# Attention plus gated MLP on one core: query blocks outermost, P V as column-tiled matmuls, and a static task-graph schedule

## The chip, the cores and the metric

One core of one Trainium2 chip. The metric is device time in microseconds (us) of the whole program, the median of several runs. The kernel before was run again beside every experiment. Its medians in those calls were 999 to 1001 us, so medians of different calls can be put side by side to about 0.2%; its single runs lie between 994.6 and 1008.4 us. The *clock* of a run is the share of the full TensorE clock that the profile records as granted.

## The reference, cut to what matters

```python
xn = layernorm(x)                                   # x: 1 x 2048 x 512
q, k, v = split(xn @ wqkv)                          # 32 heads of 16
p = softmax(q @ k.T / 4)                            # 32 heads x 2048 x 2048
attn = (p @ v) @ wo
h = relu(xn @ W_gate) * (xn @ W_up)                 # 1792 wide
out = x + attn + h @ W_down
```

The softmax takes 32 x 2048 x 2048 exponentials. Both kernels compute them on ScalarE as 683 activations of 128x1536 straight from PSUM (three PSUM banks, which I call a *unit*), and skip the maximum. A 17th column of ones in v gives the row sums. Everything that is not scores, exp or P V is *background*: projections of q, k, v, the gated MLP and the output projection. It has one PSUM bank in both kernels.

## The kernel before

Heads are taken in groups of four; for one group and one tile of 128 keys, all 2048 queries. P V has exp as the stationary operand (128x128) and v as the moving one (17 columns), and VectorE adds the result into SBUF once per head and key tile:

```python
def issue_partial(p):                  # one head, one key tile, 16 query tiles
    ...
    for m in range(NT):
        ev = PE.op(lambda e, ...: e.matmul(
            ps_pv[:, m, 0:VN], pool[:, sl, off:off + 128], v_aug[:, kt, h, 0:VN], start=True, stop=True), ...)
    ...
        eva = DV.op(lambda e, a=a: e.tensor_tensor(acc[:, a, :, 0:VN], ps_pv[:, :, 0:VN], acc[:, a, :, 0:VN], ALU.add), C_DVE)
```

Each unit issues three row-tiled score matmuls, the exp, at most one P V partial, and then about two background matmuls (a budget of 350 ns at 250 ns each):

```python
for u in range(NU):
    if u >= NS:
        PE.wait(ev_exp[u - NS])
    ...                                                       # three score matmuls, one exp
    if state["next_p"] < len(pending) and p_ulast[pending[state["next_p"]]] <= u - NS:
        issue_partial(pending[state["next_p"]])
        state["next_p"] += 1
    bg_step(u, BG_BUDGET_NS * (n / 3.0))                      # BG_BUDGET_NS = 350
```

The prologue normalises all 2048 rows and transposes them before the first exp.

The softmax here doesn't subtract the row's maximum and nothing guards it: scores larger than these inputs give would overflow.

## Time and profile before

| | us |
|---|---|
| median of the runs | 998.8 |
| profiled run | 1002.1 |
| start of the first exp | 35.6 |
| 683 exps at 1.345 each | 919 |
| time lost between exps | 28 |
| after the last exp | 20 |

The exps (one activation of a unit each) set the pace: in undisturbed stretches one starts every 1.345 us. So I read the kernel as a prologue, 683 exps at that pace, what is lost between them, and a tail.

First the page of the kernel before: span, busy time, two rows of the slices (tenths busy; the tenths of full TensorE clock that were granted), the chain that ended last, and the costliest groups (busy us, mean ns of one | idle time before them, and what ended it).

```profile
span 1002.1 us, 25305 instructions
PE 868.8 (87%) x11424; PEld 372.3 (37%) x11424; DVE 457.2 (46%) x968; ACT 944.0 (94%) x703; POOL 6.4 (1%) x8
...
ACT  5799998999999999999999999999999999999992
...
PEclk9999986899955799699995899899977575555556
...
ACT 70%; PE 21%; DVE 6%; DMA 2%; issue 1%; SPq 0%; DVEq 0%; ACTq 0%
...
L976 ACT ACTIVATE pool<-ps_sc 128x1536 bf16<-128x1536 f32 (+1 forms) x683 | 925.9, 1754 | 21.2 <-PE ps_sc L953 19.1
L917 DVE TENSOR_TENSOR acc<-ps_pv,acc 128x272 f32<-128x272 f32 x480 | 212.6, 443 | 416.0 <-PE ps_pv L904 413.6
L953 PE MATMUL ps_sc<-qTb,kTb 32*128 32x512 bf16 x2048 | 322.4, 465 | 72.4 <-ACT pool L976 68.6
L904 PE MATMUL ps_pv<-v_aug,pool 128*128 128x17 bf16 x8192 | 292.9, 173 | 2.4 <-DVE acc L917 1.7
```

ScalarE is busy 94% of the span and the chain lies on its exps. VectorE is far from full (46%). The clock row falls to half near the end and dips before.

Next, TensorE's part of the timeline: a unit with background work at full clock, then two units without at half clock (start us, duration us).

```profile
601.74 0.39 PE L953 MATMUL ps_sc<-qTb,kTb 32*128 32x512 bf16 x3 [0.41 <-ACT pool L976]
...
602.07 0.56 PE L904 MATMUL ps_pv<-v_aug,pool 128*128 128x17 bf16 x16
...
602.48 0.59 PE L511 MATMUL ps_bg<-xnT,wus 128*128 128x512 bf16 x2
...
603.09 0.39 PE L953 MATMUL ps_sc<-qTb,kTb 32*128 32x512 bf16 x3
```

```profile
860.33 0.61 PE L953 MATMUL ps_sc<-qTb,kTb 32*128 32x512 bf16 x3 [0.21 <-ACT pool L976]
...
860.87 0.59 PE L904 MATMUL ps_pv<-v_aug,pool 128*128 128x17 bf16 x16
...
861.67 0.61 PE L953 MATMUL ps_sc<-qTb,kTb 32*128 32x512 bf16 x3 [0.21 <-ACT pool L976]
```

From the start of a score group to the next matmul it is 0.32 us at full clock and 0.54 at half. In both cases the next score group comes about 1.345 us later.

### The profile page before, as it was taken

The page shows a single profiled execution, that of the slowest core. Times are in us where ns is not written, and L with a number is a line of the kernel's source. Part 1 is how long each engine was busy: PE and PEld are TensorE (multiplying, and loading weights), DVE is VectorE, ACT ScalarE, POOL GpSimd, SP SyncE. Part 2 cuts the span into 40 slices and gives each one's busy share as a digit, 9 for nine tenths or more (in the row PEclk, how much of TensorE's full clock was granted, in tenths as well). Part 3 has the DMA queues.
Part 4 walks back from the last instruction along what each step waited for, and adds up shares of the span by engine and source line. Part 5 has one row for each costly group of instructions (what it writes and reads, how often), then busy time and mean ns, then how long its engine had stood idle before and what let it go on. Part 6 is the DMA issues. An engine that isn't in the chain of part 4 may idle for free.

```text
span 1002.1 us, 25305 instructions
## 1 busy us (share of the span) xinstructions
PE 868.8 (87%) x11424; PEld 372.3 (37%) x11424; DVE 457.2 (46%) x968; ACT 944.0 (94%) x703; POOL 6.4 (1%) x8
## 2 busy tenths in 40 slices
PE   2899988999999999998989998999989987787774
PEld 1333433333343333333343333433334333343332
DVE  7455444455555335443355543445535522332226
ACT  5799998999999999999999999999999999999992
POOL 2000000000000000000000000000000000000000
PEclk9999986899955799699995899899977575555556
DMA  7000211121220002021030110212100000000002
GB/s 262 22 2 3 74 43 48 43 71 45 55 62 1 12 12 65 22 54 23 1 86 1 33 43 2 54 25 52 33 22 2 2 1 1 2 1 1 1 2 85
DMA packets 73532, 34.40 MB, mean 34 GB/s; under 512 B 60240, under 2 KB 71760, under 8 KB 73424
## 3 DMA queue, kind: packets, MB, share of 16 engines
q1 hardware_dynamic: 72272, 31.73, 11.6%
q8 instruction: 90, 1.47, 0.6%
q10 hardware_dynamic: 1152, 1.05, 0.3%
q14 instruction: 18, 0.15, 0.0%
HBM read 25.95 MB, written 6.82 MB: 33 GB/s over the span
## 4 chain that ended last, share of the span: by engine, by line
ACT 70%; PE 21%; DVE 6%; DMA 2%; issue 1%; SPq 0%; DVEq 0%; ACTq 0%
ACT pool L976 70%; PE ps_sc L953 7%; PE ps_pv L904 6%; PE ps_bg L663 2%; PE ps_bg L542 2%; PE ps_bg L524 1%; DVE acc L917 1%; DVE stats L250 1%; PE ps_bg L573 1%; DVE resb L676 1%; PE ps_bg L511 1%; PE ps_bg L639 1%; DVE stg L674 1%; DMA wus<-in_B_W_up_dram 1%; PE psT L286 1%
## 5 line engine op out<-in xcount | busy, mean ns | idle before, releaser
L976 ACT ACTIVATE pool<-ps_sc 128x1536 bf16<-128x1536 f32 (+1 forms) x683 | 925.9, 1754 | 21.2 <-PE ps_sc L953 19.1
L917 DVE TENSOR_TENSOR acc<-ps_pv,acc 128x272 f32<-128x272 f32 x480 | 212.6, 443 | 416.0 <-PE ps_pv L904 413.6
L953 PE MATMUL ps_sc<-qTb,kTb 32*128 32x512 bf16 x2048 | 322.4, 465 | 72.4 <-ACT pool L976 68.6
L904 PEld LDWEIGHTS ps_pv<-v_aug,pool 128*128 128x128 bf16 x8192 | 245.3, 99 | 157.8 <-issue 89.5
L904 PE MATMUL ps_pv<-v_aug,pool 128*128 128x17 bf16 x8192 | 292.9, 173 | 2.4 <-DVE acc L917 1.7
L953 PEld LDWEIGHTS ps_sc<-qTb,kTb 32*128 32x128 bf16 x2048 | 68.6, 94 | 357.0 <-ACT pool L976 287.5
L524 PE MATMUL ps_bg<-xnT,wgs 128*128 128x512 bf16 x224 | 70.9, 399 | 6.6 <-DVE up_sb L518 6.4
L511 PE MATMUL ps_bg<-xnT,wus 128*128 128x512 bf16 x224 | 68.8, 389 | 9.0 <-DVE hT L533 6.9
L542 PE MATMUL ps_bg<-Wd_sb,hT 128*128 128x512 bf16 x224 | 75.2, 421 | 1.0 <-DVE resb L550 1.0
L533 DVE SCALAR_TENSOR_TENSOR hT<-ps_bg,up_sb 128x512 bf16<-128x512 f32 x56 | 38.7, 691 | 20.9 <-PE ps_bg L524 20.8
L518 DVE COPY up_sb<-ps_bg 128x512 f32<-128x512 f32 x56 | 38.7, 691 | 20.7 <-PE ps_bg L511 20.6
L676 DVE TENSOR_TENSOR resb<-ps_bg,resb 128x512 f32<-128x512 f32 x48 | 33.2, 691 | 8.4 <-PE ps_bg L663 8.4
L573 PE MATMUL ps_bg<-xnT,Wk_pad 128*128 128x512 bf16 x96 | 31.7, 415 | 4.8 <-DVE stg L582 4.8
L582 DVE CAST stg<-ps_bg 128x512 bf16<-128x512 f32 x36 | 24.9, 691 | 17.9 <-PE ps_bg L573 7.2
L663 PE MATMUL ps_bg<-Wo_sb,oT_sb 128*128 128x512 bf16 x50 | 29.2, 584 | 2.9 <-DVE resb L676 2.4
L914 DVE COPY acc<-ps_pv 128x272 f32<-128x272 f32 x32 | 14.2, 443 | 26.3 <-PE ps_pv L904 26.1
L286 PE MATMUL psT<-ident,xn_buf 128*128 128x128 bf16 x64 | 9.0, 304 | 19.7 <-DVE xn_buf L278 18.3
L639 PE MATMUL ps_bg<-ident,o_sb 128*64 128x128 bf16 x116 | 22.7, 296 | 0.2
L597 PE MATMUL ps_bg<-Wv_sb,xnT 128*128 128x512 bf16 x64 | 19.2, 382 | 1.8 <-DVE v_aug L603 1.4
L511 PEld LDWEIGHTS ps_bg<-xnT,wus 128*128 128x128 bf16 x224 | 13.2, 97 | 17.7 <-DVE hT L533 11.0
L524 PEld LDWEIGHTS ps_bg<-xnT,wgs 128*128 128x128 bf16 x224 | 13.2, 97 | 14.8 <-DVE up_sb L518 10.2
L570 PE MATMUL ps_bg<-xnT,Wq_perm 128*128 128x512 bf16 x48 | 16.0, 418 | 2.5 <-DVE stg L582 2.5
(59 smaller groups left out, 199.4 us busy)
## 6 DMA issues: line engine op xcount, KB each, us to landing
wgs<-in_B_W_gate_dram SPq DMA_DIRECT2D x56, 128.0 KB, 2.3
wus<-in_B_W_up_dram SPq DMA_DIRECT2D x56, 128.0 KB, 2.8
kT_scr<-stg SPq DMA_DIRECT2D x24, 128.0 KB, 1.8
kTb<-kT_scr SPq DMA_DIRECT2D x6, 512.0 KB, 3.5
x_sb<-in_A_x_dram SPq DMA_DIRECT2D x4, 512.0 KB, 5.7
Wd_sb<-in_B_W_down_dram SPq DMA_DIRECT2D x1, 1792.0 KB, 15.1
wqkv_sb<-in_A_wqkv_dram SPq DMA_DIRECT2D x1, 1536.0 KB, 10.6
qT_scr<-stg SPq DMA_DIRECT2D x12, 128.0 KB, 1.8
```

Source lines behind the costliest of these rows:

```text
L511: fns.append(lambda e, pf, ph, dt=dt, slot=slot, sc=sc: e.matmul(pf, wus[:, slot, dt, :], xnT[:, dt, 512 * sc:512 * (sc + 1)], start=(dt = ...
L518: upj.evac = (lambda e, pf, ph, us=us: e.tensor_copy(up_sb[:, us, :], pf))
L524: fns.append(lambda e, pf, ph, dt=dt, slot=slot, sc=sc: e.matmul(pf, wgs[:, slot, dt, :], xnT[:, dt, 512 * sc:512 * (sc + 1)], start=(dt = ...
L533: gj.evac = (lambda e, pf, ph, us=us, ft=ft: e.scalar_tensor_tensor(out=hT[:, ft, :], in0=pf, scalar=0.0, in1=up_sb[:, us, :], op0=ALU.max ...
L542: fns.append(lambda e, pf, ph, ft=ft, st=st: e.matmul(pf, hT[:, ft, 128 * st:128 * (st + 1)], Wd_sb[:, ft, :], start=(ft == 0), stop=(ft = ...
L573: fns.append(lambda e, pf, ph, dt=dt, idx_=idx_, sc=sc: e.matmul(pf, Wk_pad[:, dt, idx_, :], xnT[:, dt, 512 * sc:512 * (sc + 1)], start=(d ...
L663: return [lambda e, pf, ph: e.matmul(pf, oT_sb[:, tb, mq, 128 * t:128 * (t + 1)], Wo_sb[:, gg, :], start=True, stop=True)]
L676: wj.evac = (lambda e, pf, ph, m=m: e.tensor_tensor(resb[:, m, :], pf, resb[:, m, :], ALU.add))
L904: ev = PE.op(lambda e, m=m, sl=sl, off=off, kt=kt, h=h: e.matmul(ps_pv[:, m, 0:VN], pool[:, sl, off:off + 128], v_aug[:, kt, h, 0:VN], sta ...
L917: eva = DV.op(lambda e, a=a: e.tensor_tensor(acc[:, a, :, 0:VN], ps_pv[:, :, 0:VN], acc[:, a, :, 0:VN], ALU.add), C_DVE)
L953: ev = PE.op(lambda e, bank=bank, kb=kb, qb=qb, j=j, kt=kt, c4=c4: e.matmul(ps_sc[:, bank, :], kTb[32 * j:32 * j + 32, kb, 128 * kt:128 * ...
L976: ev_exp[u] = AC.op(lambda e, s0=s0, n=n, fb=fb: e.activation(pool[:, s0:s0 + n, :], ps_sc[:, fb:fb + n, :], ACTF.Exp, scale=0.25), C_ACT)
```

## The change

Its intent: P V with v as the stationary operand (17 columns, one column tile per head) and exp as the moving one (512 queries), so that four heads sum over all key tiles inside one PSUM bank. That needs query blocks outermost, and it frees VectorE from 480 additions. Everything else is written as operations with dependencies, modelled durations and priorities. A list scheduler orders them once, at build time, and that order is each engine's program. The prologue normalises only the first 512 rows before the first exp. The diff, cut to its core:

```diff
+    def run(self):                     # Graph: the list scheduler
+        ...
+        while n < len(ops):
+            best = None
+            for e in self.ENGS:
+                pick = None
+                for o in cand[e]:
+                    at = earliest(o)
+                    ...
+                    late = at > free[e] + 1e-6
+                    key = (late, at if late else 0.0, o.prio, o.idx)   # ready ones first, then by priority
...
-        def issue_partial(p):
...
-                    ps_pv[:, m, 0:VN], pool[:, sl, off:off + 128], v_aug[:, kt, h, 0:VN], start=True, stop=True),
+                        ins = e.matmul(ps_b[32 * j:32 * j + VN, 0, :], v_aug[:, kt, 8 * gg + 2 * j + ee, 0:VN],
+                                       ring[:, UNIT * tr.slot + i, :], start=(kt == 0), stop=(kt == NT - 1), tile_position=(0, 32 * j))
...
-            bg_step(u, BG_BUDGET_NS * (n / 3.0))
+        for c4 in range(NB):
+            a = upos(c4) + (40 if c4 == 0 else 28)
+            z = upos(c4 + 1) - (12 if c4 < NB - 1 else 50)
+            for ft in range(FT):
+                later(a + (z - a) * ft / FT, 8, lambda pr, od, c4=c4, ft=ft: glu(c4, ft, pr, od))
+            for i in range(4):
+                if c4 < NB - 1:
+                    later(upos(c4 + 1) + 8 + 4 * i, 6, lambda pr, od, c4=c4, i=i: out_rows(c4, i, pr, od, range(8), True, True))
+                else:
+                    later(upos(c4, 3, 1, 0) + 8 + 4 * i, 6, lambda pr, od, c4=c4, i=i: out_rows(c4, i, pr, od, range(7), True, False))
...
+            dma(lambda e: e.dma_start(rsum[:, par, :], o_sb[DH:128:32, to.slot, :]), ...)      # row sums out of the four tiles
+            G.op("DVE", 260, lambda e: e.reciprocal(rrec[:, par, :], rsum[:, par, :]), ...)
+            dma(lambda e: e.dma_start(rec_scr[n].rearrange("j (i q) -> (j i) q", q=16), rrec[:, par, :]), ...)
+                ins = e.dma_start(rb[:, trb.slot, :], rec_scr[n].unsqueeze(1).to_broadcast([4, 32, 512]))
+            G.op("POOL", 1200, lambda e: e.tensor_tensor(oT[:, tn.slot, :], o_sb[:, to.slot, :], rb[:, trb.slot, :], ALU.mult), ...)
```

One query block is 171 units, and there are four. `glu` is 8 matmuls of up and gate; `out_rows` is 22 matmuls (14 of down, 8 of the output projection) for 128 rows.

## The prediction

> **What bounds the kernel now.** ScalarE. In the page's costliest groups the exp (683 activations of 128x1536 from PSUM) is busy 926 of 1002 us; in undisturbed stretches of the chain of waits one starts every 1.345 us (66 in 88.8 us), so the exps alone need 919 us. By the timeline the first exp starts at 35.6 us, the last ends at about 982. The span is 36 (prologue) + 919 + 28 (stalls between exps) + 20 (tail). The waits of ScalarE name score matmuls for 19 of the 28.

> **What the change does.** The exps keep count, shape and pace. Only the other 83 us can move.

> 1. P V. Before: 8192 matmuls, 128x128 weights, 17 columns moving; 16 take 0.56 us, 12 belong to a unit, so about 0.40 us of PE a unit, and 480 additions on VectorE (213 us). After: 2048 matmuls of 512 columns, three in different column tiles. Row-tiled scores show three at once: 0.32 us a group at full clock, 0.54 at half. If column tiles overlap as well [...], P V costs 0.3 us a unit. VectorE loses 200 us of work, but it isn't the bound, so that gives almost nothing directly. PE load at full clock: 0.32 + 0.32 + 0.28 (216 background matmuls of 0.22 us per 171 units) = 0.92 of 1.345 us.
> 2. Background work is spread over the whole run. The granted clock, 0.85 mid-run and 0.5 after 800 us by the windows, should stay at 0.85 or more. At half clock the load would be 1.6 us a unit, over the exp's pace, so cold stretches cost. I expect stalls of 12 us in steady state, down from 28.
> 3. Prologue. LayerNorm in blocks of 512 rows, no late table loads, no permuted weight copies. From measured pieces: x lands at 4.9, four bn_stats 2.4, power on GpSimd 1.2, normalise and transpose 2.5, copy-out 1, q 2, k mask 1.5, score 0.5: first exp at 16.5 instead of 35.6 us, 19 saved.
> 4. But the first 21 units run through all 16 key tiles in 29 us, and VectorE must normalise three more blocks (7.3 us each) and evacuate v (16 x 0.69): about 37 us of VectorE from 4.9 us on, needed by 38. I expect 7 us of stall: part of the prologue comes back.
> 5. Tail: the division now goes through three small DMAs of about 2 us each and a GpSimd multiply, but only four output tiles remain instead of 16: 16 instead of 20 us.

> **Sum.** 16.5 + 919 + 7 + 12 + 16 = 970 as profiled; the median before is 3 us below its profile, so 967 us, 80% range 952 to 985. Faster by over 2%: 0.78; within 2%: 0.17; slower by over 2%: 0.05.

> **What would show the steps.** First exp near 16.5 us; exp waits before 45 us naming k masks or scores; VectorE busy near 250 us; P V groups of three near 0.32 us; clock 0.85 or more to the end; exp pace unchanged; 16 us after the last exp.

> **What would make it wrong.** Column tiles that run one after another (0.65 us a unit: PE bound, over 1000 us). [...] The clock falling to half. A fixed PE order waiting for a late VectorE evacuation of the one P V bank or the one background bank.

Before the run nothing showed that column tiles overlap; the 0.3 us of step 1 was an estimate from the 0.32 us of the score groups. The 1.2 us of step 3 for the power on GpSimd is in no trace of the kernel before; the changed kernel took 1.02 us for it (L448).

## The result, and the profile after

The changed kernel takes 1047.5 us (median of 4) against 1000.9: **4.8% slower** (ratio 1.048, 95% interval 1.044 to 1.052). The prediction was 967 us.

The page of the changed kernel, with the lines that answer to those above:

```profile
span 1044.5 us, 11864 instructions
PE 863.8 (83%) x5152; PEld 205.5 (20%) x5152; DVE 191.1 (18%) x323; ACT 932.4 (89%) x687; POOL 51.1 (5%) x46
...
ACT  3699999999889999999988999999998899999980
...
PEclk9998896976599777878569887787758989895587
...
ACT 58%; PE 33%; DMA 4%; DVE 3%; issue 1%; POOL 0%; POOLq 0%; SPq 0%
...
L711 ACT ACTIVATE ring<-ps_sc 128x1536 bf16<-128x1536 f32 (+1 forms) x683 | 929.2, 1555 | 69.6 <-PE ps_sc L699 55.0
L699 PE MATMUL ps_sc<-qT,kT 32*128 32x512 bf16 x2048 | 318.0, 460 | 133.3 <-ACT ring L711 126.4
L729 PE MATMUL ps_b<-ring,v_aug 128*17 128x512 bf16 x2048 | 304.3, 455 | 1.2 <-DVE o_sb L663 1.2
```

VectorE lost its 266 us of work as intended. ScalarE does the same exps, but sits idle 69.6 us before them, 55.0 of it waiting for score matmuls. The clock row now wavers all through the run.

I split the span by the starts of the exps, read from the trace. "Lost" is the time from one start to the next, less 1.345 us, summed.

| | before | predicted | after |
|---|---|---|---|
| first exp starts at | 35.6 | 16.5 | 21.2 |
| exps at 1.345 us | 919 | 919 | 919 |
| lost up to 60 us | -0.3 | 7 | 10.8 |
| lost after 60 us | 27.9 | 12 | **67.5** |
| after the last exp | 20.0 | 16 | 26.6 |
| span | 1002.1 | 970 | 1044.5 |

Every term missed upwards, but one carries most of the error: 67.5 us instead of 12. The following part of the timeline of the changed kernel shows how it is lost.

```profile
405.25 0.40 PE L729 MATMUL ps_b<-ring,v_aug 128*17 128x512 bf16 x3
...
405.58 0.60 PE L500 MATMUL ps_b<-xnT,wgs 128*128 128x512 bf16 x2
...
409.56 0.39 PE L699 MATMUL ps_sc<-qT,kT 32*128 32x512 bf16 x3 [0.63 <-ACT ring L711]
409.88 0.39 PE L729 MATMUL ps_b<-ring,v_aug 128*17 128x512 bf16 x3
...
412.24 0.61 PE L699 MATMUL ps_sc<-qT,kT 32*128 32x512 bf16 x3 [0.63 <-ACT ring L711]
412.78 0.60 PE L729 MATMUL ps_b<-ring,v_aug 128*17 128x512 bf16 x3
...
414.67 1.03 PE L500 MATMUL ps_b<-xnT,wus 128*128 128x512 bf16 x2
415.63 0.61 PE L699 MATMUL ps_sc<-qT,kT 32*128 32x512 bf16 x3
416.17 0.60 PE L729 MATMUL ps_b<-ring,v_aug 128*17 128x512 bf16 x3
416.70 1.03 PE L500 MATMUL ps_b<-xnT,wus 128*128 128x512 bf16 x2
417.67 0.61 PE L699 MATMUL ps_sc<-qT,kT 32*128 32x512 bf16 x3
...
418.33 2.94 ACT L711 ACTIVATE ring<-ps_sc 128x1536 bf16<-128x1536 f32 x2 [0.59 <-PE ps_sc L699]
```

The same stretch in windows (columns after the length: busy time and instructions of PE, PEld, DVE, ACT, POOL, then granted clock, DMA share, GB/s):

```profile
410.00:412.00 2.00, 0.98 (x9) 0.19 (x6) 0.00 (x0) 2.00 (x2) 0.00 (x0) 1.00 0.14 32
412.00:414.00 2.00, 1.55 (x9) 0.31 (x9) 0.00 (x0) 2.00 (x3) 0.00 (x0) 0.54 0.17 38
414.00:416.00 2.00, 2.00 (x11) 0.33 (x8) 0.00 (x0) 2.00 (x2) 0.00 (x0) 0.50 0.00 0
416.00:418.00 2.00, 2.00 (x11) 0.33 (x8) 0.23 (x1) 1.67 (x2) 0.00 (x0) 0.50 0.00 0
```

A P V group takes 0.32 us at full clock, as predicted (from 405.25 to the next matmul at 405.58; the trace's nanoseconds give a median of 0.323; with one column tile for all heads it is 0.748, in e8 below), so the column tiles do overlap. Two such groups in a row take 0.535 us, so one more group adds 0.21 us (an estimate from the two medians). What the other 0.11 us consists of, no run shows. But then for five units there is no background work, TensorE idles half of each unit (busy 0.98 of the 2 us from 410), and the clock falls to half at 412. The next background matmuls come at 414.67 and run at half clock: a unit now needs 0.54 + 0.54 + 0.97 = 2.05 us. The score groups at 415.63 and 417.67 are 2.04 us apart, and ScalarE waits 0.59 us before the exp at 418.33.

Counting background matmuls between successive score groups, in the order in which TensorE's program holds them, for units 343 to 513 of each kernel, which in the changed kernel and its edits are the third query block (one digit a unit; the last two kernels are experiments told below):

```
before  222222222222221111111111111111222222222222222222222222222222222222220022222222222222222222222222222222222222222222222222222222222222222222222222222222222222222222002222222
after   000000002644606446226446464480422004400022220000002222000002222220002222000000222200000222200000222200000422220000022220000022220000002222000002222220000000000000000000000
e5      000000002112112112112112112112112112112112112112112112112112112112112112112112112112112112112112112112112112112112112112112112112112112112112112112112112112112112112112110
e6      222222222222222222222222222222222222222222222222222222222222222222222222222222222222222222202222222202222222222222222220222222220222222222022222222222222222222222222222222
```

The old loop gave nearly every unit two, until its background work ran out at unit 559 (after it only 8 units and the tail have any). The scheduler spreads the *jobs* evenly, but each job runs as soon as it is ready: *bursts* (several background matmuls in one unit) and *lulls* (units in a row with none). Sorting the units after 60 us by the clock granted during them and by background matmuls started in them (half clock: over 80% of the unit at half; full clock: under 10%):

| units by clock and background | before: units, lost us | after: units, lost us |
|---|---|---|
| half clock, none | 120, -0.9 | 141, -1.7 |
| half clock, some | 129, 24.1 | 93, **51.7** |
| clock changes within the unit | 15, 4.8 | 41, 5.2 |
| full clock, none | 16, -0.2 | 150, -2.2 |
| full clock, 1 or 2 | 326, -1.2 | 150, -1.5 |
| full clock, 3 or more | 57, 1.4 | 86, **16.0** |

The tail lost 10 us to two things, shown by the end of the timeline:

```profile
1020.40 0.83 PE L729 MATMUL ps_b<-ring,v_aug 128*17 128x512 bf16 x12
...
1025.90 1.03 PE L729 MATMUL ps_b<-ring,v_aug 128*17 128x512 bf16 x14
...
1026.97 0.69 DVE L663 COPY o_sb<-ps_b 128x512 f32<-128x512 f32 x1 [0.28 <-PE ps_b L729]
...
1031.23 0.54 SPq L677 DMA_DIRECT2D rb<-rec_scr  x1
1036.42 1.26 POOL L681 TENSOR_TENSOR oT<-o_sb,rb 128x512 bf16<-128x512 f32 x1 [38.20 <-DMA rb<-rec_scr]
```

The last exp ended at 1017.9, but the last P V matmuls stood behind `out_rows` in TensorE's order and ran until 1026.9. And the broadcast DMA took 5.2 us until the multiply, where I had allowed 2. The first statistics of the prologue started at 7.25 us, 2.3 us later than the 4.9 that the prediction took from the kernel before:

```profile
1.36 5.71 DVE L371 TENSOR_SCALAR pid<-pid 128x2 int32<-128x2 int32 x1
...
3.24 3.81 POOL L383 MEMSET Wo_p<- 128x4096 bf16 x1
...
7.25 1.28 DVE L442 BATCH_NORM_STATS2 stats<-x_sb 128x6 f32<-128x512 bf16 x2
```

A VectorE instruction on two columns ended at 7.07, just after GpSimd's memsets did (7.05); the statistics queue behind it. It took 5.71 us here and 0.16 in e7, where the memsets come after it. In e7 another, on 128x4 elements, took 1.24 us beside the big memset, against 0.17 in e11, where that memset comes later. Statistics instructions took 0.66 us each in e7 beside that memset, and 0.66 here after it.

### The profile page after: what moved, and what is told of

It reads as the page before. It is cut to its first block, busy times and chain, and to the rows that moved or that the text cites. A ratio compares the mean times of both kernels' runs of the same rounds, so it can differ in the third digit from the quotient of the medians. Undisturbed runs are those within 1.5% of the kernel's fastest.

```text
span 1044.5 us, 11864 instructions
## 1 busy us (share of the span) xinstructions
PE 863.8 (83%) x5152; PEld 205.5 (20%) x5152; DVE 191.1 (18%) x323; ACT 932.4 (89%) x687; POOL 51.1 (5%) x46
## 4 chain that ended last, share of the span: by engine, by line
ACT 58%; PE 33%; DMA 4%; DVE 3%; issue 1%; POOL 0%; POOLq 0%; SPq 0%
ACT ring L711 58%; PE ps_b L500 18%; PE ps_sc L699 9%; PE ps_b L729 6%; DMA rb<-rec_scr 2%; DMA rsum<-o_sb 1%; DMA rec_scr<-rrec 1%; DMA wus<-in_B_W_up_dram 1%; DVE stats L442 1%; DVE pid L371 1%; DVE v_aug L533 0%; POOL oT L681 0%; PE ps_sc L500 0%; DVE o_sb L663 0%; DVE kT L525 0%
## 5 line engine op out<-in xcount | busy, mean ns | idle before, releaser
L711 ACT ACTIVATE ring<-ps_sc 128x1536 bf16<-128x1536 f32 (+1 forms) x683 | 929.2, 1555 | 69.6 <-PE ps_sc L699 55.0
L699 PE MATMUL ps_sc<-qT,kT 32*128 32x512 bf16 x2048 | 318.0, 460 | 133.3 <-ACT ring L711 126.4
L729 PE MATMUL ps_b<-ring,v_aug 128*17 128x512 bf16 x2048 | 304.3, 455 | 1.2 <-DVE o_sb L663 1.2
L699 PEld LDWEIGHTS ps_sc<-qT,kT 32*128 32x128 bf16 x2048 | 68.0, 93 | 442.4 <-ACT ring L711 342.6
L729 PEld LDWEIGHTS ps_b<-ring,v_aug 128*17 128x17 bf16 x2048 | 61.8, 89 | 199.4 <-issue 187.6
L595 DVE COPY up_sb<-ps_b 128x512 f32<-128x512 f32 x56 | 38.7, 691 | 315.7 <-PE ps_b L500 315.7
L500 PE MATMUL ps_b<-xnT,wus 128*128 128x512 bf16 x224 | 90.8, 505 | 1.8 <-DMA wus<-in_B_W_up_dram 1.7
L681 POOL TENSOR_TENSOR oT<-o_sb,rb 128x512 bf16<-128x512 f32 x32 | 40.5, 1266 | 956.4 <-DMA rb<-rec_scr 927.1
L500 PE MATMUL ps_b<-xnT,wgs 128*128 128x512 bf16 x224 | 73.8, 421 | 1.9 <-DMA wgs<-in_B_W_gate_dram 0.5
L500 PE MATMUL ps_b<-Wd,hT 128*128 128x512 bf16 x224 | 63.8, 414 | 8.0 <-POOL oT L681 6.3
L500 PEld LDWEIGHTS ps_b<-Wd,hT 128*128 128x128 bf16 x224 | 18.4, 101 | 40.5 <-issue 16.0
L500 PEld LDWEIGHTS ps_b<-xnT,wgs 128*128 128x128 bf16 x224 | 13.8, 99 | 35.3 <-DVE up_sb L595 19.4
L512 DVE CAST qT<-ps_b 128x512 bf16<-128x512 f32 x15 | 10.3, 689 | 30.6 <-PE ps_b L500 30.6
```

Of the source, the lines that this page charges most:

```text
L500: ins = e.matmul(bank_of(tile, sub), l(), r(), start=(i == 0), stop=(i == n - 1))
L512: G.op("DVE", 690, lambda e: e.tensor_copy(qT[:, tq.slot, :], bank_of(t, sub)), reads=[t], writes=[tq], prio=prio)
L595: G.op("DVE", 690, lambda e: e.tensor_copy(up_sb[:, tup.slot, :], bank_of(tu)), reads=[tu], writes=[tup], prio=pr)
L681: G.op("POOL", 1200, lambda e: e.tensor_tensor(oT[:, tn.slot, :], o_sb[:, to.slot, :], rb[:, trb.slot, :], ALU.mult), reads=[to, trb], wri ...
L699: ins = e.matmul(ps_sc[:, 3 * ts.slot + i, :], kT[32 * j:32 * j + 32, 2 * gg + ee, 128 * kt:128 * kt + 128], qT[32 * j:32 * j + 32, t_q[(c ...
L711: return e.activation(ring[:, UNIT * tr.slot:UNIT * tr.slot + n, :], ps_sc[:, 3 * ts.slot:3 * ts.slot + n, :], ACTF.Exp, scale=0.25)
```

## The experiments

Theory A: lulls without background work let the clock fall, and the next burst pays. Rival B: the bursts alone, whatever the clock. Rival C: column tiles, or changes of tiling mode, cost TensorE time. All experiments are edits of the changed kernel, except e12. All but e8 gave a correct result.

| run | median us | ratio to before, 95% | clock | first exp | lost to 60 / after | tail |
|---|---|---|---|---|---|---|
| changed kernel | 1047.5 | 1.048 (1.044-1.052) | 0.805 | 21.2 | 10.8 / 67.5 | 26.6 |
| e1_fill | 1002.4 | 1.002 (0.995-1.008) | 0.986 | 21.4 | 9.6 / 25.9 | 26.4 |
| e2_spread | 1042.2 | 1.042 (1.036-1.048) | 0.876 | 21.6 | 9.6 / 69.8 | 22.6 |
| e3_cap | 1034.4 | 1.034 (1.028-1.040) | 0.833 | 21.2 | 10.8 / 59.5 | 19.7 |
| e4_ends | 1028.1 | 1.028 (1.022-1.033) | 0.811 | 19.8 | 9.6 / 60.5 | 18.0 |
| e5_spread2 | 983.9 | 0.985 (0.981-0.990) | 0.961 | 21.6 | 9.6 / 7.9 | 23.6 |
| e6_cap_fill | 974.4 | 0.976 (0.972-0.979) | 0.995 | 21.4 | 9.6 / 3.1 | 20.1 |
| e7_all | 965.0 | 0.966 (0.963-0.970) | 0.996 | 20.5 | 6.4 / -1.8 | 18.1 |
| e8_serial | 1085.0 | 1.086 (1.082-1.090) | 0.994 | 21.6 | 15.1 / 97.6 | 30.6 |
| e9_short_fill | 1050.4 | 1.050 (1.047-1.054) | 0.801 | 21.6 | 9.6 / 74.1 | 26.5 |
| e10_fill_one | 1005.9 | 1.007 (1.004-1.010) | 0.974 | 21.5 | 9.5 / 29.2 | 26.4 |
| e11_all2 | 964.0 | 0.965 (0.962-0.968) | 0.991 | 17.3 | 8.5 / -1.8 | 18.4 |
| e12_before_fill | 994.3 | 0.995 (0.992-0.998) | 0.906 | 35.6 | -0.3 / 18.8 | 19.4 |

### e1_fill: more work in the lulls

After scheduling, a pair of matmuls whose result nobody reads goes into each stretch between two score groups that holds no background matmul and in which the background bank is free:

```diff
         G.run()
+        def filler(e):
+            for i in range(2):
+                ins = e.matmul(ps_b[:, 1, :], Wd[:, 2 * i, 0:128], Wd[:, 2 * i + 1, :], start=True, stop=True)
+            return ins
+        G.fill(P_b, 1, filler, 440)      # into every such stretch of TensorE's order
         G.emit(nc, es)
```

> The changed kernel with a pair of extra matmuls, whose result nobody reads, put into every stretch between two score groups that holds no background matmul (273 pairs) wherever the background bank is free; nothing else moves. Theory A (the clock): in stretches without background work the granted clock falls to half, and the next burst of background work then runs at half clock and holds the exps up (units at half clock with background work cost 52 of the 78 us lost between exps). Then MORE work on TensorE makes the kernel FASTER: mean clock from 0.80 to over 0.92, loss of units at half clock with background work from 52 to under 15 us, time 1047 to about 1005-1015 us. Rival B (the fixed order: too many background matmuls between two score groups, whatever the clock): the bursts stay as they are, time within 1% of 1047. Rival C (cost of column tiles or of changing the tiling mode, TensorE short of time): more work on TensorE makes it slower, over 1055.

Measured: 1002.4 us, 45 us less with more work for TensorE, at a clock of 0.986. The loss after 60 us fell from 67.5 to 25.9. Units at half clock, or in which it changes, now lose 10.4 us instead of 56.9; units at full clock with 3 or more background matmuls still lose 18.2. Rival C is out, and B cannot be the main part. The clock row of its page:

```profile
PEclk9999999999999999999999999999999999999997
```

### e9_short_fill: the control

```diff
-                ins = e.matmul(ps_b[:, 1, :], Wd[:, 2 * i, 0:128], Wd[:, 2 * i + 1, :], start=True, stop=True)
+                ins = e.matmul(ps_b[:, 1, 0:16], Wd[:, 2 * i, 0:128], Wd[:, 2 * i + 1, 0:16], start=True, stop=True)
```

> A control for the fill run: the same pairs of unread matmuls in the same places, but 16 columns moving instead of 512 (weights 128x128 as there). If the clock answers to how long the array streams, these pairs give next to nothing: clock about 0.80 to 0.83, time 1035-1050, as the changed kernel. If it answers to the presence of instructions or to shorter idle gaps, or if the pairs help for a reason other than the clock (they sit in the order and shift it), time falls to about 1002 as in the fill run.

Measured: 1050.4 us at a clock of 0.801: nothing gained, if anything a little lost. As many instructions in the same places do not help: with 512 columns each (e1) the clock was 0.986. What helped is the time that they stream.

```profile
PEclk9998898966598687777559978788658988995577
```

### e10_fill_one: half the dose

```diff
-            for i in range(2):
+            for i in range(1):
```

> Half the dose: one unread matmul of 512 columns in each of the same places. A lull unit then streams 0.64 us of 1.345 at full clock (score group 0.21, P V group 0.21, one matmul 0.21) instead of 0.43 without and 0.85 with a pair. It shows where the clock falls. In the evenly dealt run, 1.33 matmuls a unit kept the clock at full in 528 of 547 units with work, so one matmul should mostly suffice: clock 0.93 to 0.98, time 1003-1015. If the clock needs more than that: 0.85 and 1025-1040.

Measured: 1005.9 us, clock 0.974. One matmul of 512 columns in a lull unit is nearly enough. At full clock a matmul of 512 columns takes about 0.215 us (in the changed kernel four in a row take 0.969 us up to the next score group and two take 0.538; the difference is two). I estimate from this, counting a score group and a P V group, three matmuls at once each, as one each: a lull unit of the changed kernel streams 2 x 0.215 of its 1.345 us (32%), and there the clock fell (0.805 over the run); with one more matmul it is 48%, and it mostly held (0.974).

### e2_spread: dealing the background out, with a mistake

Each score group placed earns a credit of background matmuls, at most 2 saved; a background operation is a candidate only if its credit is there. `mm_chain` emits single matmuls instead of pairs.

```diff
+                    if o.name == "bg" and o.prio >= 0 and left_sc and credit < o.dur / 220:
+                        continue
...
+            if o.name[:2] == "sc":
+                credit = min(CAP, credit + RATE)
+                left_sc -= 1
+            elif o.name == "bg" and o.prio >= 0:
+                credit -= o.dur / 220
...
+            if best is None and left_sc and credit < CAP:     # nothing else can be placed: lift the ration
+                credit = CAP
+                continue
```

> The changed kernel with its background matmuls dealt out evenly by the scheduler: each score group placed earns 1.35 background matmuls, at most 2 are saved up, so that nearly every unit holds 1 or 2 (no bursts, hardly any lulls). (This file still lets the q projections wait their turn behind other background work, so a clump of 9 stands before four score groups.) Theory A (clock): clock over 0.92, loss between exps after the first 60 us from 67 to under 20 us, time 990-1005. Rival B (bursts alone) expects about the same here; the next run tells A from B. Rival C (column tiles cost): the same work in all, so within 1% of 1047.

Measured: 1042.2 us, a miss. (The file was built with 1.4, not 1.35.) By priority the q projection of the next head group stood behind all other background work. With that held to its ration, the scores came to need a q that was not there, and the scheduler let everything ahead of it run at once: three gaps of 15.4, 17.1 and 15.7 us, each holding 45 or 46 background matmuls. Those cost 44 us beyond three exps. The clock, 0.876, missed theory A's forecast of over 0.92 too: with 1.4 matmuls a unit the work of a block ran out before its end, and 53 units at half clock with background work lost 28.4 us. That doesn't contradict A: elsewhere 368 units ran at full clock with 1 or 2 background matmuls and lost nothing.

### e3_cap: bursts cut, lulls left

The same limiter with a credit of 2 a unit and pairs of matmuls, so bursts of more than two vanish but the lulls stay.

> The changed kernel with bursts cut to at most 2 background matmuls between two score groups, but not dealt out: they still come in runs, with lulls of 5 to 28 units between. Theory A (clock): lulls still bring half clock, so units at half clock with background work still lose 20-40 us; time 1015-1035, clearly slower than the evenly dealt run. Rival B (bursts alone): same as the evenly dealt run, 990-1005. Rival C: 1047.

Measured: 1034.4 us, with the same fault as e2 (three gaps of 9.7 us, 25 us in all beyond the exps). Leaving those out, units at half clock with background work still lose 35.8 us, and units at full clock nothing. So cutting bursts alone does not remove the loss: against rival B.

### e5_spread2: dealing out, mended

```diff
-                    later(upos(c4, gg) - 16, 8, lambda pr, od, c4=c4, gg=gg: proj_q(c4, gg, pr, order=od))
+                    later(upos(c4, gg) - 16, 8, lambda pr, od, c4=c4, gg=gg: proj_q(c4, gg, 0.01, order=od))
```

plus the limiter of e2 with 1.35.

> The evenly dealt run again, mended: in the first one the q projections waited behind other background work, and three score groups stood 15 to 17 us behind clumps of 45 matmuls (about 44 us). Now they come first, and each score group earns 1.35 matmuls (the first one was built with 1.4, not 1.35 as its expectation says). Lulls of 9 to 22 units remain at the block boundaries. Theory A (clock): clock about 0.88, cold units with background work lose 20-28 us, time 992-1002. If dealing out were useless (the extra matmuls of the first run helped for another reason than the clock), time stays above 1030.

Measured: 983.9 us, better than expected, with no extra matmul at all: the same work as the changed kernel in another order, 6% faster. 528 units ran at full clock with 1 or 2 background matmuls. The loss after 60 us is 7.9 us net; 14 units at half clock with background work make 10.6 of it, and the units at full clock give a few back (they run at 1.338).

### e6_cap_fill: both at once

The limiter of e3, q first, and the filler of e1.

> Bursts cut to 2 background matmuls a unit, q projections first, and every remaining stretch without background work filled with the unread pair, so that nearly every unit holds exactly 2. If clock (about 45 us, seen in the fill run) and bursts (about 18 us at full clock plus 12 us of P V starved behind them at block boundaries) are separate and add up: loss after the first 60 us from 67 to under 8 us, time 1047 to 978-986. If the bursts cost nothing once the clock is up: 1002 as in the fill run.

Measured: 974.4 us, clock 0.995, 3.1 us lost after 60 us. So the bursts cost something of their own once the clock is up: from e1 to this run the loss fell by 22.8 us. That the two costs simply add is not shown, for cutting the bursts alone (e3, without its three gaps) had already taken 33 us off. The tail fell by 6.3 us, because 10 background matmuls and not 32 now stand between the last exp and the last P V.

### e4_ends: prologue and tail alone

```diff
-        G.op("POOL", 4200, lambda e: e.memset(Wo_p[:], 0.0), writes=[t_woz], prio=-400)
+        G.op("POOL", 4200, lambda e: e.memset(Wo_p[:], 0.0), reads=t_masks, writes=[t_woz], prio=-400)
...
-                ins = e.dma_start(rb[:, trb.slot, :], rec_scr[n].unsqueeze(1).to_broadcast([4, 32, 512]))
+            for j in range(4):
+                dma(lambda e, j=j: e.dma_start(rb[32 * j:32 * j + 32, trb.slot, :], rec_scr[n, j].unsqueeze(0).to_broadcast([32, 512])), ...)
...
-                     writes=[tp], prio=u + PV_LAG, name="pv%d" % u)
+                     writes=[tp], prio=u + PV_LAG - (1000 if u > NU - 30 else 0), name="pv%d" % u)
...
-                    later(upos(c4, 3, 1, 0) + 8 + 4 * i, 6, ... range(7), True, False))
+                    later(NU - 40 + 8 * i, 2, ... range(6), True, False))
```

> The changed kernel with its ends mended and its middle left: (1) GpSimd's two big memsets wait for the VectorE mask instructions, one of which ended only with those memsets at 7.07 us; first bn_stats at about 5 instead of 7.25, first exp at about 19 instead of 21.2. (2) The broadcast of the reciprocals as four DMAs of 32 partitions in place of one whose outermost dimension is 4: landing 2 to 3 us instead of 5.2, so the three waits of TensorE for the scaled output (6.3 us, up to 3.3 each) at the block boundaries go mostly. (3) The last P V matmuls before the background work of the last block, and that work begun earlier: last P V within 2 us of the last exp instead of 8, tail from 26.6 to about 16. In sum 1047 to about 1022-1030 us if these costs are separate and on the path; if stalls in the middle absorb them, above 1035.

Measured: 1028.1 us, 19 us less. The tail fell from 26.6 to 18.0 us and the first exp came 1.4 us earlier. The time from the issue of the broadcast to the multiply fell from a median of 5.1 to 3.5 us, and the waits of TensorE for the scaled output at block boundaries from 6.3 to 2.4 us. The middle kept its clock troubles (60.5 us lost).

### e7_all and e11_all2: everything together

e7 is e6 with the ends of e4, and with v evacuated behind the k masks in the first pass (the first 21 units, which run through all 16 key tiles). e11 moves the big memset behind the first pass of v and puts the second block's statistics behind the first block's normalisation:

```diff
-            proj_v(kt, -690 + 10 * (kt // 4) + 0.1 * kt, allowed=(0, 1) if kt < 8 else (1,))
+            proj_v(kt, (-674 if kt < 4 else -660) + 0.1 * kt, allowed=(0, 1) if kt < 8 else (1,))   # e7
...
+        G.op("POOL", 4200, lambda e: e.memset(Wo_p[:], 0.0), reads=[t_v[NT - 1]], writes=[t_woz], prio=-400)   # e11
...
+                G.op("DVE", 620, lambda e, m=m: e.bn_stats(...), ..., order=last_xn[:] if b == 1 else ())          # e11
```

> The capped and filled run plus the mended ends (masks before the memsets, four broadcast DMAs, last P V first) plus the evacuation of v moved behind the k masks of the first pass (k of all four blocks first), against the 9.6 us lost in the first 60 us. Ends gave 19 us alone (first exp 1.4 earlier, tail 8.6 shorter, 7 us in the middle, of which capping takes part). Expected: first exp 19.8, loss in the first 60 us 3-6 us, after that under 8, tail 16-18: 960-970 us, so 3 to 4% below the kernel before the change. If v is too late for P V, the ring of exps fills instead and the first 60 us lose as much as before: 966-974.

> The capped, filled and mended run with a better prologue: the memset of the output weights comes after the first pass of v (it held a VectorE instruction of the first block up from 6.3 to 7.5 us), and the statistics of the second block stand behind the normalisation of the first (VectorE waited 1.9 us for the second block's data while the first was ready). First exp 20.5 to about 17 us. VectorE has the same work before the keys of the first pass are complete, so 0 to 3 us of it come back as stall in the first 60 us (6.4 now). Time 965 to 960-964 us.

Measured: e7 965.0 us and e11 964.0 us, 3.4 and 3.5% faster than the kernel before and 8% faster than the changed kernel as it came. The two cannot be told apart. The first exp of e11 comes at 17.3 us, but 8.5 instead of 6.4 us are lost in the first 60 us. From e7's page:

```profile
span 962.2 us, 12618 instructions
...
PEclk9999999999999999999999999999999999999998
```

After 60 us, e7 runs a shade faster than 1.345 us an exp. What is left above 919 us is prologue, the first pass and the tail.

### e8_serial: what column tiles are worth

All four heads in column tile 0, which gives a wrong result (the bank is also preset to ones and not zeros):

```diff
-                        ins = e.matmul(ps_b[32 * j:32 * j + VN, 0, :], ...
-                                       ..., start=(kt == 0), stop=(kt == NT - 1), tile_position=(0, 32 * j))
+                        ins = e.matmul(ps_b[0:VN, 0, :], ...
+                                       ..., start=(kt == 0 and j == 0), stop=(kt == NT - 1 and j == 3), tile_position=(0, 0))
```

> The changed kernel with all four heads' P V matmuls in column tile 0 (wrong result on purpose: four heads sum into the same rows), so that no two can run at once; count, shapes and order stay. It measures what column tiling is worth and tests the step of the prediction that P V in tiles costs 0.32 us a group of three. Expected: groups of three take 0.65 us at full clock and 1.28 at half instead of 0.32 and 0.54; TensorE needs 1.25 us of 1.345 a unit on average, over it in every unit with background work: time 1090-1150. If column tiles did not overlap in the changed kernel anyway, time stays at 1047.

Measured: 1085.0 us, a little under the range of 1090 to 1150. Its timeline:

```profile
405.50 0.39 PE L699 MATMUL ps_sc<-qT,kT 32*128 32x512 bf16 x3
405.82 0.81 PE L729 MATMUL ps_b<-ring,v_aug 128*17 128x512 bf16 x3
```

From the start of a P V group to the next matmul it takes 0.748 us against 0.323 in the changed kernel, both at full clock. The clock was 0.994 with this longer P V, against 0.805, so the run loses by TensorE's time alone. Column tiling is worth 38 us even against a kernel with a bad clock.

### e12_before_fill: the same remedy for the old kernel

```diff
+            n_ops = len(PE.items)
             bg_step(u, BG_BUDGET_NS * (n / 3.0))
+            if len(PE.items) == n_ops and bg["active"] is None and can_start(u, True):
+                PE.wait(bgalloc["last_done"].get(next_bank()))
+                pf = bank_views[next_bank()][0]
+                for i in range(2):
+                    PE.op(lambda e, pf=pf, i=i: e.matmul(pf, Wd_sb[:, 2 * i, 0:128], Wd_sb[:, 2 * i + 1, :], start=True, stop=True))
```

> The kernel BEFORE the change with unread pairs of 512-column matmuls into the background bank in every unit in which it has no background work (all of the last 170 units among others). It lost 28 us between exps, 24 of them in units at half clock with background work. If that is the clock: clock 0.81 to over 0.93, loss to 5-12 us, time 1000 to 980-990. If its cold units come from its own lulls of TensorE inside stretches WITH background work (waiting for VectorE or a DMA), the pairs don't reach them: clock up after 800 us only, time within 1% of 1000. Either way it tells how much of the gain of the mended kernel is the change's own: the mended one needs 20 us to its first exp, this one 36.

Measured: 994.3 us, 0.5% less, clock 0.906; the loss after 60 us went from 27.9 to 18.8. Between the two branches: the clock is now up after 800 us (0.96), but 90 units with 1 or 2 matmuls still run at half clock (15.6 us lost), in stretches that had background work all along. In six of the run's 7 falls before the last exp, the background matmuls were transposes of 128 columns (L640 of this kernel), which the table counts like any other. In the trace of the kernel before, four of the ten falls between 60 us and the last exp came right after such transposes (at 406.8, 526.2, 642.3 and 761.8). No run takes the transposes out, so what takes the clock down there is not shown. The mended kernel (964) beats this one by 30 us, of which 15 to 18 are its earlier first exp, about 20 the loss after 60 us; 7 to 9 of that come back as loss in the first pass.

## Why the prediction was wrong

- **The bound and the floor: right.** ScalarE's exps kept count and pace (1.345 us); in e7, all 657 unit steps after 60 us lose nothing in sum (-1.8 us), all of them at full clock.
- **P V in column tiles (step 1): right.** A group takes 0.32 us at full clock, as named; with all heads in one column tile it takes 0.748 (e8), 2.3 times as long. VectorE fell to 191 us busy (250 named); no run tests what that alone is worth.
- **The clock (step 2): wrong, and this is the step that failed.** I wrote that background work "is spread over the whole run", so that the clock "should stay at 0.85 or more" and steady-state stalls come to 12 us. Measured: clock 0.805, stalls 67.5 us. Two errors sit in it. I averaged the background over 171 units (0.28 us each), where the order holds it in bursts of 2 to 8 matmuls a unit, with lulls of up to 6 units inside a block and of 28 to 30 across the borders of blocks. And I gave half clock a cost of "1.6 us a unit", from that same average, where a half-clock unit with two background matmuls needs 2.05 us. The diff held both facts: each job has one position, and a ready operation runs at once. The prediction did list "the clock falling to half" among what would make it wrong, but gave "slower by over 2%" a chance of only 0.05. e1 shows the clock to be the cause of about 42 us (67.5 to 25.9), close to the 51.7 of the table less the 8.2 of the block borders; e9 shows that it was streaming and not the number of instructions that kept it up (clock 0.801 with pairs of 16 columns, 0.986 with 512 in e1); e5 shows that the same work dealt out evenly does without the loss.
- **Bursts at full clock:** not in the prediction. 16 us in units with 3 or more background matmuls; e6 took them off.
- **First exp: 16.5 named, 21.2 measured.** The missing terms: VectorE held until 7.07 us by the instruction beside GpSimd's memsets (5.71 us, 0.16 in e7), and orders that assumed earlier data. e11 reaches 17.3 with those mended, so the chain of pieces itself was sized about right.
- **First pass: 7 us named, 10.8 measured.** The mechanism was named (VectorE's work before the keys are complete). In e11 an exp that starts 3.2 us earlier loses 2.1 us more, which fits it; that VectorE's work is the sole limit is argued, not shown.
- **Tail: 16 named, 26.6 measured.** I took the last P V to follow the last exp at once, where it started 8 us later, behind 32 matmuls of output work, and three DMAs of 2 us, where the third takes 5. e4 brings the tail to 18.0.

Nearly all of what was lost is the order, not the arithmetic: e5, without any extra matmul, takes 983.9 us. With the same P V, another order, mended ends and unread matmuls in the lulls, the kernel runs at 964 us. That this is close to the 967 predicted is luck: it is another schedule, and its first exp, first pass and tail all cost a little more than named, while its stalls cost 14 us less.

## What to carry to other kernels

When TensorE is not the bound but feeds the engine that is, look at its work unit by unit and not on average: count the matmuls between two waits, and deal background work out so that every unit streams enough to keep the clock up and no unit holds more than fits (here 983.9 us in e5 against 1047.5, with the same work). The static order, built from full-clock durations, made bursts and lulls whose cost its model did not show; where lulls cannot be avoided, matmuls whose result nobody reads can pay for themselves (here 1002.4 us in e1). Check the ends of a static order by hand: the last critical operation should not queue behind work that nobody waits for.
